# Six more seven-product groups, gates and casts on GpSimd, and a written-out priority table in a fused attention and gated-MLP kernel

## Chip, cores and metric

The kernel runs on one core of a Trainium2 chip. The metric is the time of one execution on the device, in microseconds (us). A ratio is the time of the changed kernel over the time of the kernel before.

## What is computed

Linear attention with a cosine reweighting, then a two-layer network whose gate is h cos(h). Inputs are float32; the kernel computes in float16 and accumulates in float32.

```python
# q, k, v: (8 batches, 8 heads, 576 tokens, 64)
def phi(x, c, s):
    r = np.maximum(x, 0.0)
    return np.concatenate([r * c, r * s], axis=-1)
q_p = phi(q, cos_w, sin_w)
k_p = phi(k, cos_w, sin_w)
kv = np.einsum('bhsf,bhsd->bhfd', k_p, v)
z = np.sum(k_p, axis=2)
num = np.einsum('bhsf,bhfd->bhsd', q_p, kv)
den = np.einsum('bhsf,bhf->bhs', q_p, z)[..., None] + 1e-06
x = num / den          # as 4608 tokens x 512
h = x @ w_in           # 512 -> 2048
out = (h * np.cos(h)) @ w_out   # 2048 -> 512
```

## The kernel before

**Stages.** The 4608 tokens are worked in nine chunks of 512: chunk c below 8 takes 512 tokens of batch c, and the last, chunk 8, collects the 64 left over of each batch. For a chunk there are three stages. `attention(c)` (L1061) loads k, q and v, scales and rectifies them (`prep`, L419 on ScalarE or L420 on VectorE), casts v to float16 (`cast_v`, L433 or L434), multiplies (L446, L507) and normalises (`norm`, L523 to L527). `layer1(c)` (L584) multiplies by w_in and gates. `layer2(c)` (L864) multiplies by w_out; its TensorE work runs interleaved with `layer1(c + 1)`. Chunks 0 and 1 use plain forms of layer 1 (L604), chunk 0 also of layer 2 (L834).

**A plain group of layer 1** (`layer1_plain`, L630) is four tiles of 128 hidden units by 512 tokens. Each tile is four matmuls 512 wide (L636) into one PSUM bank and a `gate`: ScalarE takes the sine of h plus pi/2 (L577), and VectorE multiplies it by the bank (L579).

**A seven-product group** (`layer1_fast`, L708) makes the same four tiles as a 2x2 block product with seven block products instead of eight. Each product is four matmuls 256 wide (L740), so a group has 28 of them against 16 of twice the width. It needs sums of w_in blocks (`w_in_sums`, L669, VectorE) and of x blocks (`layer1_sums`, L689, VectorE). Partial results leave PSUM by three ScalarE copies (L748) into SBUF tiles Y, U and Z and three VectorE additions onto them (L752). Y is gated from SBUF (L577, L579). U and Z are gated together, 1024 wide, from SBUF (L763, L769). The fourth tile is gated from PSUM. `FAST1` (L643) says how many of the four groups of a chunk are done so: two in each of chunks 3 to 8, twelve groups in all. A second set of w_in sums, for groups 2 and 3, is made only if some chunk has more than two (`LATE`, L652); it lies in the buffers of qT.

**Layer 2 from chunk 1 on** is also a seven-product scheme (L897), with sums of the gated tiles on VectorE (L879, L924), copies on ScalarE (L908) and additions on VectorE (L912). In the last chunk the seventh product goes on accumulating in bank A, and at the end ScalarE copies one half of that bank (L943) and VectorE the other (L945), both under one key, and `store` sends the two halves of the tokens from the SP and ACT queues.

**What sets the order.** Every step is given to `Plan` (L18) with an engine, a cost, a due time and the keys that it reads and writes. `Plan.run` (L73) repeats a forward list schedule over the costs (`forward`, L110) and a backward pass that makes new priorities from it, with random changes, and keeps the shortest. The instructions are then issued in the order of the planned starts; each engine works its own in that order, and waits are by semaphores. Steps marked `port=True` (the SBUF sums, `prep`, `cast_v`, gates that name an engine) are kept apart in the plan between VectorE and GpSimd (`held`, `other`, L125 to L132); at run time nothing but the order does this. A gate or `mul` takes VectorE or, with `pool` true, GpSimd (L564). `Y_POOL` and `UZ_POOL` (L645) are empty, so no gate is on GpSimd, and the plan prices one there at 3.4 times the VectorE cost (L569).

**GpSimd's queue** carries the loads of w_in (L976) and w_out (L990), tiny copies that hold back a load until another tensor has landed (L970, L980, L995, L1002), and the output stores (L803) of chunks 0 to 7, each waiting for its rows. `hold2` (L979) keeps the first half of w_out back until the second quarter of w_in has landed.

Of the kernel before, what the change touches and what calls it, by code (L numbers as in the profile page):

```python
# [3 lines left out]

# [7 lines left out]
AF = mybir.ActivationFunctionType  # L12
# [2 lines left out]
F16 = mybir.dt.float16  # L15


class Plan:  # L18

    LINK = {"PE": 0.12, "ACT": 0.05, "DVE": 0.05, "POOL": 0.1, "SP": 0.0}

    PASSES, ROUNDS = 12, 117  # L30


    SHARE, WAKE, LAND = {"HW": 0.40, "SW": 0.56}, {"HW": 1.1, "SW": 1.3}, 1.0
# [7 lines left out]

    def add(self, eng, occ, lat, due, fn, rd=(), wr=(), dma=None, lane=None, late=0.0,
            lazy=None, port=False):

        n = len(self.steps)
        prev = self.lanes.get(lane)
        if lane is not None:  # L50
            self.lanes[lane] = n
        deps = set()
        for key in rd:
            if key in self.wr:
                deps.add(self.wr[key])
        for key in wr:
            if key in self.wr:
                deps.add(self.wr[key])
            deps.update(self.rd.get(key, ()))
        for key in rd:  # L60
            self.rd.setdefault(key, []).append(n)
        for key in wr:
            self.wr[key] = n
            self.rd[key] = []
        deps.discard(n)
        opts = [(eng, occ, lat, fn)] if isinstance(eng, str) else eng
        self.steps.append(dict(opts={o[0]: o for o in opts}, due=due,
                               deps=deps, dma=dma, n=n, prev=prev, late=late,
                               lazy=lazy, port=port))
        self.steps[n].update(zip(("eng", "occ", "lat", "fn"), opts[0]))  # L70
        return n

    def run(self):  # L73

        best = [math.inf]
        rnd = random.Random(1)

        def passes(key, n):
            local = None
            for _ in range(n):
                start, done = self.forward(key)
                end = max(done)
                if end < best[0]:
                    best[:] = [end, start, done, [s["eng"] for s in self.steps]]
                key = self.backward(start, done, end)
                if local is None or end < local[0]:
                    local = end, key  # L90
            return local
        now = passes([s["due"] for s in self.steps], self.PASSES)
        for _ in range(self.ROUNDS):
            amp, wide = rnd.choice((0.5, 1, 2, 4)), rnd.choice((20, 40, 80, 300))
            mid = rnd.uniform(0, best[0])
            key = [k + (rnd.gauss(0, amp) if abs(k - mid) < wide / 2 else 0) for k in now[1]]
            new = passes(key, 4)
            if new[0] < now[0] + 0.02:
                now = new
        for s, a, b, e in zip(self.steps, *best[1:]):  # L100
            s["start"], s["end"] = a, b
            s.update(zip(("eng", "occ", "lat", "fn"), s["opts"][e]))
        return sorted(self.steps, key=lambda s: (s["start"], s["n"]))

    def link(self, n, u):
        st = self.steps
# [3 lines left out]
    def forward(self, key):  # L110
# [103 lines left out]
                late = wake + (self.BUSY if r == "HW" and rings["SW"] and not rings["HW"] else 0.0)  # L214
                rings[r].append([late, s["dma"][0] / s["dma"][1], n, wake])
        return start, done

    def backward(self, start, done, end):
        st = self.steps
        left = [0] * len(st)  # L220
        for s in st:
            for d in s["deps"]:
                left[d] += 1
            if s["prev"] is not None:
                left[s["prev"]] += 1
        limit = [end - done[n] + start[n] for n in range(len(st))]
        late = [0.0] * len(st)
        free = {e: end for e in self.LINK}
        ready = {e: [] for e in self.LINK}
        for n, k in enumerate(left):  # L230
            if not k:
                ready[st[n]["eng"]].append(n)
        for _ in st:
            best = None
            for e, cand in ready.items():
                if not cand:
                    continue
                at = {n: min(free[e], limit[n] + st[n]["occ"]) for n in cand}
                top = max(at.values()) - self.PATIENCE.get(e, 0.0)
                k, t, n = max((start[n], at[n], n) for n in cand if at[n] >= top)  # L240
                if best is None or t > best[0]:
                    best = (t, e, n)
            t, e, n = best
            ready[e].remove(n)
            late[n] = free[e] = t - st[n]["occ"]
            for d in st[n]["deps"]:
                limit[d] = min(limit[d], late[n] - self.link(d, n) - (done[d] - start[d]))
                left[d] -= 1
                if not left[d]:
                    ready[st[d]["eng"]].append(d)  # L250
            d = st[n]["prev"]
            if d is not None:
                limit[d] = min(limit[d], late[n] - 0.01)
                left[d] -= 1
                if not left[d]:
                    ready[st[d]["eng"]].append(d)
        return late


@with_exitstack  # L260
def kernel(
# [162 lines left out]
    def cast_v(b, t, eng, due, hs=slice(0, H), nt=1):  # L424
# [4 lines left out]
            in_ = raw["v"][:, :, t:t + nt, :]  # L429
        rd, wr = hk("v", heads), [("V1", t + i, h) for h in heads for i in range(nt)]  # L430
        f = nt * len(heads) / H
        cost = {"DVE": 0.09 + 0.33 * f, "ACT": 0.12 + 0.5 * f, "POOL": 0.9}
        fn = {"ACT": lambda: nc.scalar.activation(out=out_, in_=in_, func=AF.Copy),  # L433
              "DVE": lambda: nc.vector.tensor_copy(out=out_, in_=in_),  # L434
              "POOL": lambda: nc.gpsimd.tensor_copy(out=out_, in_=in_)}
# [128 lines left out]
    def mul(due, cost, fn, rd, wr, pool):  # L564

        if pool is None:
            dve(cost, due, lambda: fn(nc.vector), rd, wr)
        elif pool:
            pl.add("POOL", 3.4 * cost, 0.15 + 3.4 * cost, due, lambda: fn(nc.gpsimd), rd, wr,  # L569
                   port=True)  # L570
        else:
            dve(cost, due, lambda: fn(nc.vector), rd, wr, port=True)
# [67 lines left out]
             rd=["KQ"] if c == B else [])  # L640


    FAST1 = {3: 2, 4: 2, 5: 2, 6: 2, 7: 2, 8: 2}  # L643
    SUMS_AT = min(FAST1) - 1
    Y_POOL, UZ_POOL = (), ()  # L645
    CH2, JF = NCT // 2, JH * P // 2


# [156 lines left out]
    def store(c, h, o, due, fs=None):  # L805
        O = ost[o]
        keys = [("ost", o, f) for f in range(2)]
        if c < B:
# [2 lines left out]
            put(due, five[:, 2 * h:2 * h + 2, :], blocks(O, n), keys, nc.gpsimd, "POOL")  # L811
            put(due, four[:, 2 * h:2 * h + 2, :], blocks(O, 1 - n), keys, nc.gpsimd, "POOL")
            return
        for n in range(2):
            f = slice(0, Dm) if fs is None else slice(fs * MH, (fs + 1) * MH)
            dst = out.rearrange("(i n s) m -> n i s m", n=2, s=S)[n][2 * h:2 * h + 2, 0:S5, f]
            put(due, dst.rearrange("i (p t) m -> p t i m", t=NT + 1)[:, NT], blocks(O, n)[:, :, f],
                keys if fs is None else [("ost", o, fs)],
                *((nc.scalar, "ACT") if n else (nc.sync, "SP")), nb=262.0 if fs is None else 131.0)

    def layer2_plain(c):

# [41 lines left out]
    def layer2(c):  # L864
# [22 lines left out]
        C_ = Bk if c < B else BANKS[2]  # L887
        order = iter(range(1, 8))

        def product(bank, a, b, rd, first, last):  # L890
            n = next(order)
            for tt in range(2):
                due = w0 + (n - 0.5 + 0.5 * tt) / 7 * ww * 0.97

                def mm(tt=tt):
                    for j in range(JH):
                        nc.tensor.matmul(  # L897
                            bank[0][:, tt * MH:(tt + 1) * MH], lhsT=a[:, j, tt * P:(tt + 1) * P],
                            rhs=b[:, j, :], start=(first and tt == 0 and j == 0),
                            stop=(last and tt == 1 and j == JH - 1), skip_group_check=True)  # L900
                pe(JH, MMH, due, mm, rd, [bank[1]])
            return due

# [31 lines left out]
        store(c, 0, ol, d + 1.5)  # L935
        if c == B:
            store(c, 1, oh, d + 1.0, 1)
        d = product(A, a22, T4, gk(1, 1) + ["T4"], False, True)
        if c < B:
            copy(ost[oh][:, :, m0], A, [("ost", oh, 0)], d + 0.5)  # L940
            store(c, 1, oh, d + 1.5)
        else:
            act(0.3, d, lambda: nc.scalar.activation(  # L943
                out=ost[oh][:, 0, m0], in_=view(A)[:, 0], func=AF.Copy), [A[1]], [("ost", oh, 0)])
            dve(0.33, d, lambda: nc.vector.tensor_copy(  # L945
                out=ost[oh][:, 1, m0], in_=view(A)[:, 1]), [A[1]], [("ost", oh, 0)])
            store(c, 1, oh, d + 1.0, 0)


    def setup():  # L950
        nc.gpsimd.memset(S2[:, 0:2, :], 0.5)
# [16 lines left out]
    def weights():  # L968
# [10 lines left out]
        def hold2():  # L979
            nc.gpsimd.tensor_copy(  # L980
                out=w_out_sb[0:1, :, 0].rearrange("p (g j) -> p g j", g=4)[:, :, 0],
                in_=w_in_sb[0:1, 0, Dff // 4:Dff // 4 + 1].broadcast_to((1, 4)))
        if W_FIRST is None:
            pl.add("POOL", 0.2, 0.3, 0, hold2, [("w_in", 1)], [("w_out", g) for g in range(4)])
            w_out_load(0, 2)

    def w_out_load(g0, g1):
        for g in range(g0, g1):
            js = slice(g * NJT // 4, (g + 1) * NJT // 4)
            pl.add("POOL", 0.9, 0, 0, lambda js=js: nc.gpsimd.dma_start(  # L990
                out=w_out_sb[:, js, :], in_=wo[:, js, :]), (), [("w_out", g)], dma=(1048.0, 400.0), late=LATE_W)

    def hold_raw(nm):
        for h in (0, HB) if nm == ORDER1[2] else (0,):
# [66 lines left out]
    def attention(b):  # L1061
# [4 lines left out]
            for g in range(2):  # L1066
                prep(b, "k", t, g, "", T + 1.2 * t)
        for t, nt in ((0, 2), (2, 2), (4, 1)):
            cast_v(b, t, "", T + 6 + 0.4 * t, nt=nt)
        kv(b, T + 8)  # L1070
        for t in range(NT + 1):
            due = T + 8 + 1.2 * t
# [71 lines left out]
```

## Time and profile before

| | |
|---|---|
| median of 3 timed runs | 285.62 us (284.65 to 286.38) |
| span of the profiled execution | 282.8 us |
| median less span | 2.8 us |
| PE, DVE, ACT, POOL busy | 272.4, 247.5, 215.5, 26.0 us |
| PE, DVE, ACT busy from 105 to 200 us | 94.9, 91.5, 89.3 of 95 us |
| PE busy from 0 to 60 us | 54.7 of 60 us |
| last matmul ends | 277.93 us |
| last store lands | 281.34 us |

The span runs from the first to the last instruction of one execution. The profile gives no time of that execution beyond its span, so the 2.8 us between span and median are carried over as they are. PE is TensorE's matmuls, PEld its weight loads, DVE VectorE, ACT ScalarE, POOL GpSimd, SP the queue that issues most loads. A line "L636 PE MATMUL out<-in shapes x184 | 45.9, 379 | 0.0" reads: line 636 of the code, 184 instructions recorded, 45.9 us busy, 379 ns each, and the idle time of the engine ahead of them. A PE matmul's duration includes the pipeline, so matmuls overlap; the rate at which they pass is read from rows of the timeline or the chain that hold several in one piece. A few matmul records are missing from the trace.

### The profile page before, as it was taken

The numbers are of one execution on the slowest core, as the hardware profiler recorded it, in microseconds if no ns is written. First come the engines' busy times: TensorE is split into PE (matmuls) and PEld (weight loads), VectorE is DVE, ScalarE is ACT, GpSimd is POOL, SyncE is SP. The second block draws the span as 40 slices with busy tenths as digits, with TensorE's granted clock in tenths as the row PEclk, the third lists the DMA queues.
The fourth block names the chain that finished last, engine by engine and source line by source line (L and its number), as shares of the span: only waits on it lengthen the run. The fifth ranks groups of instructions, "written<-read, shape, count | busy, mean of one in ns | idle before, by whom it ended". The sixth has DMA issues, their size and how long they took to land.

```text
span 282.8 us, 6578 instructions
## 1 busy us (share of the span) xinstructions
PE 272.4 (96%) x2619; PEld 208.3 (74%) x2619; DVE 247.5 (88%) x458; ACT 215.5 (76%) x367; POOL 26.0 (9%) x53
## 2 busy tenths in 40 slices
PE   7889989999999999999999999999999999999993
PEld 2468856669866688777877887787777877876882
DVE  2986878999999999999999999999899999967941
ACT  2947897999999999999999999995834666456420
POOL 1412020011000020002000200020002001100200
PEclk9999999999999999999999999999999999999999
DMA  6999999799989999999997899786024001100124
GB/s 214 303 204 273 258 310 300 251 270 212 344 222 240 228 227 362 170 245 224 254 268 186 265 290 224 164 159 167 2 56 168 21 2 75 76 2 0 68 82 150
DMA packets 77567, 53.30 MB, mean 188 GB/s; under 512 B 46048, under 2 KB 75232, under 8 KB 77536
## 3 DMA queue, kind: packets, MB, share of 16 engines
q1 hardware_dynamic: 70032, 39.73, 55.7%
q0 software_dynamic: 6784, 12.59, 17.1%
q10 hardware_dynamic: 720, 0.57, 0.6%
q8 instruction: 20, 0.33, 0.5%
q14 instruction: 11, 0.09, 0.1%
HBM read 36.74 MB, written 9.44 MB: 163 GB/s over the span
## 4 chain that ended last, share of the span: by engine, by line
PE 84%; DMA 8%; ACT 3%; DVE 2%; issue 1%; SPq 0%; ACTq 0%; DVEq 0%
PE M L897 33%; PE M L636 16%; PE M L740 8%; PE M L604 8%; PE TR L740 4%; PE M L834 4%; DMA vm<-in_v_dram 4%; PE TR L636 3%; PE ATT L507 3%; DMA qT<-KQ 3%; PE ATT L446 3%; DMA qm<-in_q_dram 2%; ACT KQ L419 1%; PE M L475 1%; DVE x L527 1%
## 5 line engine op out<-in xcount | busy, mean ns | idle before, releaser
L577 ACT ACTIVATE ch<-M 128x512 f32<-128x512 f32 x90 | 52.8, 595 | 11.1 <-PE M L604 4.1
L897 PEld LDWEIGHTS <-gT 128*128 128x128 f16 x560 | 53.7, 98 | 9.3
L579 DVE TENSOR_TENSOR gT<-M,ch 128x512 f16<-128x512 f32 x83 | 55.4, 683 | 4.7 <-ACT ch L577 4.2
L897 PE MATMUL M<-w_out_sb,gT 128*128 128x256 f16 x448 | 54.9, 273 | 0.0
L636 PE MATMUL M<-xT,w_in_sb 128*128 128x512 f16 x184 | 45.9, 379 | 0.0
L419 ACT ACTIVATE KQ<-qm,CS 128x512 f16<-128x512 f32 x59 | 40.1, 718 | 4.5 <-DMA qm<-in_q_dram 4.5
L419 ACT ACTIVATE KQ<-km,CS 128x512 f16<-128x512 f32 x56 | 38.3, 719 | 0.0
L636 PEld LDWEIGHTS <-w_in_sb 128*128 128x128 f16 x256 | 24.4, 98 | 18.3
L803 POOL DMA_DIRECT2D out_dram<-ost x32 | 17.0, 537 | 213.9 <-DVE ost L912 134.8
L897 PE MATMUL M<-T,S 128*128 128x256 f16 x256 | 32.5, 273 | 0.0
L604 PE MATMUL M<-xT,w_in_sb 128*128 128x256 f16 x256 | 30.6, 273 | 0.1
L897 PEld LDWEIGHTS <-S 128*128 128x128 f16 x256 | 24.9, 98 | 4.0
L604 PEld LDWEIGHTS <-w_in_sb 128*128 128x128 f16 x256 | 24.5, 98 | 3.9 <-issue 0.3
L908 ACT ACTIVATE ost<-M 128x512 f32<-128x512 f32 x31 | 18.5, 597 | 10.2 <-PE M L897 10.1
L527 DVE TENSOR_TENSOR x<-ATT,rec 128x512 f16<-128x512 f32 x32 | 22.1, 691 | 1.1
L740 PEld LDWEIGHTS <-w_in_sb 128*128 128x128 f16 x192 | 18.5, 98 | 4.9 <-issue 0.2
L912 DVE TENSOR_TENSOR ost<-M,ost 128x512 f32<-128x512 f32 x24 | 16.4, 681 | 4.0 <-issue 3.5
L507 PEld LDWEIGHTS <-qT 128*128 128x128 f16 x320 | 15.1, 98 | 4.7 <-issue 0.5
L752 DVE TENSOR_TENSOR Z<-M,Z 128x512 f32<-128x512 f32 x23 | 15.6, 684 | 2.3 <-PE M L740 1.9
L879 DVE TENSOR_TENSOR S<-gT 128x2048 f16<-128x2048 f16 (+1 forms) x16 | 17.3, 1085 | 0.2
L748 ACT ACTIVATE Z<-M 128x512 f32<-128x512 f32 x19 | 11.3, 596 | 6.6 <-PE M L740 6.4
L740 PEld LDWEIGHTS <-WS 128*128 128x128 f16 x144 | 13.6, 98 | 3.3 <-issue 0.2
(130 smaller groups left out, 421.8 us busy)
## 6 DMA issues: line engine op xcount, KB each, us to landing
out_dram<-ost POOLq DMA_DIRECT2D x32, 256.0 KB, 4.3
qm<-in_q_dram SPq DMA_DIRECT2D x8, 640.0 KB, 5.8
km<-in_k_dram SPq DMA_DIRECT2D x8, 640.0 KB, 7.8
qm<-in_q_dram SPq DMA_DIRECT2D x8, 512.0 KB, 5.6
km<-in_k_dram SPq DMA_DIRECT2D x8, 512.0 KB, 6.7
vm<-in_v_dram SPq DMA_DIRECT2D x6, 640.0 KB, 6.4
vm<-in_v_dram SPq DMA_DIRECT2D x6, 512.0 KB, 5.9
w_in_sb<-in_moe_w_in_dram POOLq DMA_DIRECT2D x4, 512.0 KB, 8.9
```

The costliest lines, as they stand in the source:

```text
L419: fn = {"ACT": lambda: nc.scalar.activation(out=out_, in_=in_, func=AF.Relu, scale=sc), "DVE": lambda: nc.vector.tensor_scalar(out=out_, i ...
L507: nc.tensor.matmul(bank[hb][:, hh * D1:(hh + 1) * D1], lhsT=a[:, h, :], rhs=z[:, h, :], start=(i == 0), stop=(i == len(parts) - 1))
L527: nc.vector.tensor_tensor(out=split(x16[n][:, hs, :], k), in0=A[:, :, :, 0:D], in1=split(rec[n][:, hs], k).unsqueeze(3).broadcast_to((P, k ...
L577: act(0.5, due, lambda: nc.scalar.activation(out=ch[c], in_=bank, func=AF.Sin, bias=math.pi / 2.0, scale=1.0), [key], [("ch", c)])
L579: mul(due, 0.61, lambda q: q.tensor_tensor(out=dst, in0=bank if len(dst.shape) == 2 else bank.rearrange("p (j s) -> p j s", j=dst.shape[1] ...
L604: nc.tensor.matmul(M1[m][:, jj * 2 * P:(jj + 1) * 2 * P], lhsT=w_in_sb[:, cc, j * P:(j + 1) * P], rhs=X[:, cc, ts], start=(cc == 0), stop= ...
L636: nc.tensor.matmul(M, lhsT=w_in_sb[:, cc, j * P:(j + 1) * P], rhs=X[:, cc, :], start=(cc == 0), stop=(cc == NCT - 1))
L740: nc.tensor.matmul(bank[0][:, j * TH:(j + 1) * TH], lhsT=a(cc, j), rhs=b[:, cc, :], start=(first and j == 0 and cc == 0), stop=(last and j ...
L803: pl.add(eng, 0.9 if eng == "POOL" else 0.65, 0, due, lambda: q.dma_start(out=dst, in_=src_), keys, [], dma=(nb, 355.0))
L879: dve(0.07 + 1.07 / NG, due, lambda: nc.vector.tensor_tensor(out=out_[:, sl], in0=a[:, sl], in1=b[:, sl], op=op), rd, wr, port=True)
L897: nc.tensor.matmul(bank[0][:, tt * MH:(tt + 1) * MH], lhsT=a[:, j, tt * P:(tt + 1) * P], rhs=b[:, j, :], start=(first and tt == 0 and j == 0),
L908: act(0.5, due, lambda: nc.scalar.activation(out=dst, in_=view(bank), func=AF.Copy), [bank[1]], dk)
```

## The change

- `FAST1` has two groups in chunks 2 to 6 and four in chunks 7 and 8: eighteen instead of twelve. So the first w_in sums are made one chunk earlier (`SUMS_AT`), and the second set (`LATE`) is made.
- `Y_POOL` and `UZ_POOL` name chunks 2 to 8: the gate of Y (512 wide) and that of U and Z (1024 wide) of all eighteen groups go to GpSimd. The plan's price of such a step changes.
- `cast_v` of batches 2 to 7 goes to GpSimd, eighteen casts.
- In the last chunk the seventh product goes to the two banks of BANKS2, one for each half of the tokens, after a ScalarE copy of what bank A holds; VectorE adds each bank to the copy, and `store_tile` sends each half by itself.
- `hold2` waits for the first quarter of w_in, and the plan takes a later landing for w_out.
- The search is gone: `run` makes one forward schedule from a written-out table `KEYS` of priorities, one for each step.

```diff
+KEYS = (
...
+)
     def run(self):
...
+        st = self.steps
+        assert len(KEYS) == len(st)
+        start, done = self.forward([k / 100 for k in KEYS])
+        for s, a, b in zip(st, start, done):
             s["start"], s["end"] = a, b
-            s.update(zip(("eng", "occ", "lat", "fn"), s["opts"][e]))
-        return sorted(self.steps, key=lambda s: (s["start"], s["n"]))
+        return sorted(st, key=lambda s: (s["start"], s["n"]))
...
-        cost = {"DVE": 0.09 + 0.33 * f, "ACT": 0.12 + 0.5 * f, "POOL": 0.9}
+        cost = {"DVE": 0.09 + 0.33 * f, "ACT": 0.12 + 0.5 * f, "POOL": 0.1 + 0.5 * f}
...
-            pl.add("POOL", 3.4 * cost, 0.15 + 3.4 * cost, due, lambda: fn(nc.gpsimd), rd, wr,
+            pl.add("POOL", 0.15 + 1.9 * cost, 0.3 + 1.9 * cost, due, lambda: fn(nc.gpsimd), rd, wr,
                    port=True)
...
-    FAST1 = {3: 2, 4: 2, 5: 2, 6: 2, 7: 2, 8: 2}
+    FAST1 = {2:2,3:2,4:2,5:2,6:2,7:4,8:4}
     SUMS_AT = min(FAST1) - 1
-    Y_POOL, UZ_POOL = (), ()
+    Y_POOL, UZ_POOL = range(2, 9), range(2, 9)
...
+    def store_tile(o, i, due):
+        for n in range(2):
+            dst = out.rearrange("(i n s) m -> n i s m", n=2, s=S)[n][2 + i, 0:S5, 0:MH]
+            put(due, dst.rearrange("(p t) m -> p t m", t=NT + 1)[:, NT], blocks(ost[o], n)[:, i, 0:MH],
+                [("ost", o, 0, i)], *((nc.scalar, "ACT") if n else (nc.sync, "SP")), nb=65.5)
...
-        d = product(A, a22, T4, gk(1, 1) + ["T4"], False, True)
         if c < B:
+            d = product(A, a22, T4, gk(1, 1) + ["T4"], False, True)
             copy(ost[oh][:, :, m0], A, [("ost", oh, 0)], d + 0.5)
             store(c, 1, oh, d + 1.5)
-        else:
-            act(0.3, d, lambda: nc.scalar.activation(
-                out=ost[oh][:, 0, m0], in_=view(A)[:, 0], func=AF.Copy), [A[1]], [("ost", oh, 0)])
-            dve(0.33, d, lambda: nc.vector.tensor_copy(
-                out=ost[oh][:, 1, m0], in_=view(A)[:, 1]), [A[1]], [("ost", oh, 0)])
-            store(c, 1, oh, d + 1.0, 0)
-
+            return
+        copy(ost[oh][:, :, m0], A, [("ost", oh, 0, i) for i in range(2)], d + 0.5)
+        d = product(BANKS2, a22, T4, gk(1, 1) + ["T4"], True, True, True)
+        for i, (bank, key) in enumerate(BANKS2):
+            dst = ost[oh][:, i, m0]
+            dve(0.33, d, lambda dst=dst, bank=bank, i=i: nc.vector.tensor_tensor(
+                out=dst, in0=bank[:, i * MH:(i + 1) * MH], in1=dst, op=ALU.add), [key, ("ost", oh, 0, i)],
+                [("ost", oh, 0, i)])
+            store_tile(oh, i, d + 1.0)
...
-                in_=w_in_sb[0:1, 0, Dff // 4:Dff // 4 + 1].broadcast_to((1, 4)))
+                in_=w_in_sb[0:1, 0, 0:1].broadcast_to((1, 4)))
         if W_FIRST is None:
-            pl.add("POOL", 0.2, 0.3, 0, hold2, [("w_in", 1)], [("w_out", g) for g in range(4)])
+            pl.add("POOL", 0.2, 0.3, 0, hold2, [("w_in", 0)], [("w_out", g) for g in range(4)])
...
-                out=w_out_sb[:, js, :], in_=wo[:, js, :]), (), [("w_out", g)], dma=(1048.0, 400.0), late=LATE_W)
+                out=w_out_sb[:, js, :], in_=wo[:, js, :]), (), [("w_out", g)], dma=(1048.0, 400.0), late=1.8)
...
-            cast_v(b, t, "", T + 6 + 0.4 * t, nt=nt)
+            cast_v(b, t, "POOL", T + 6 + 0.4 * t, nt=nt)
```

## Prediction

> **What bounds the kernel now.** I read the page's busy times first, then busy times by stretch, then the chain of waits through a middle stretch. The two lines from the page:
>
> ```profile
> PE 272.4 (96%) x2619; PEld 208.3 (74%) x2619; DVE 247.5 (88%) x458; ACT 215.5 (76%) x367; POOL 26.0 (9%) x53
> PEclk9999999999999999999999999999999999999999
> ```
>
> Three engines are near full, so shares don't decide. The clock is full throughout. Busy time by stretch (length, then PE, PEld, DVE, ACT, POOL):
>
> ```profile
> 0.00:60.00 60.00, 54.74 (x540) 38.12 (x541) 47.04 (x111) 44.36 (x77) 10.09 (x23) 1.00 1.01 261
> ...
> 105.00:200.00 95.00, 94.89 (x952) 75.53 (x950) 91.52 (x158) 89.32 (x152) 6.35 (x12) 1.00 0.91 224
> ...
> 222.00:250.00 28.00, 28.00 (x229) 22.19 (x228) 25.50 (x43) 15.97 (x28) 2.11 (x4) 1.00 0.13 44
> 250.00:278.00 28.00, 27.93 (x227) 21.96 (x225) 19.77 (x30) 12.64 (x22) 2.12 (x4) 1.00 0.12 46
> ```
>
> PE is idle for 5.3 us up to 60 us and hardly at all later, while VectorE stands at 96% from 105 to 200 us and ScalarE at 94%. Busy matmuls overlap, so I check the rate in the chain (start, length, what; PE work alone here):
>
> ```profile
> 130.56 0.87 PE M L897 x8
> 131.43 1.21 PE ATT L446 x40
> 132.64 1.75 PE M L897 x16
> 134.39 0.87 PE M L740 x8
> ...
> 145.36 1.73 PE M L636 x8
> ```
>
> Each piece starts where the one before ends. A matmul 256 wide passes in 0.87 / 8 = 0.109 us, one 512 wide in 1.73 / 8 = 0.216. TensorE runs at its own rate without holes from 60 to 277.9 us. So matmul work that goes away is time, as long as the other engines keep up.
>
> **The change part by part.** The sum is made against the profiled span, 282.8 us. The median of the runs is 285.62, so 2.8 us are added at the end unchanged.
>
> **Six more seven-product groups.** One plain group is 16 matmuls of 0.216 = 3.46 us; one seven-product group is 28 of 0.109 = 3.05. That is 0.40 us less each, 2.4 us for six, all on the full TensorE stream. Gain: **2.4 us**.
>
> Beside it, ScalarE does three copies (0.60 each), the sines of Y (0.63) and of UZ (1.06) and one sine from PSUM (0.59), 4.1 us, against four sines of 0.595, 2.4 us: 1.7 more per group, 10 in all. Two groups fall in chunk 2 (about 80 to 105 us, where ScalarE is busy 24.1 of 25) and four after 200 us, where it has 40% and more free. VectorE does three additions (0.684) and one gate (0.683) against four gates: no change, if Y and UZ are gated elsewhere.
>
> **Gates to GpSimd.** These rows show what leaves VectorE, and GpSimd's nearest row:
>
> ```profile
> L769 DVE TENSOR_TENSOR gT<-Z,ch 128x1024 f16<-128x1024 f32 x9 | 10.9, 1217 | 0.1
> ...
> L579 DVE TENSOR_TENSOR gT<-Z,ch 128x512 f16<-128x512 f32 x9 | 6.1, 682 | 0.0
> ...
> L951 POOL MEMSET S<- 128x512 f16 x1 | 0.5, 524 | 0.3 <-POOLq L1128 0.3
> ```
>
> With the three of each in other buffers, twelve groups free 12 x (1.22 + 0.68) = 22.8 us of VectorE. No row has a two-input product on GpSimd. Its floor is VectorE's own time, 0.68 and 1.22 us. For the upper end I take one memset for each of the two inputs and the output: 3 x 0.52 = 1.6 us for Y and 3.1 for UZ. I take the upper end, since the memset is GpSimd's only wide row. Eighteen groups are then 18 x 4.7 = 85 us.
>
> [...]
>
> **Casts to GpSimd.** Twelve of 1024 and six of 512 leave ScalarE (8.5 + 2.5 = 11.0 us) and VectorE (2.7 + 0.8 = 3.5). On GpSimd, one memset each for input and output: 2.1 and 1.05 us as upper end, 0.69 and 0.42 (VectorE's rows) as floor. At most 31 us. With 17 us of stores GpSimd has 133 us of the 200 from chunk 2 on, and in chunks 7 and 8 four groups take 19 us of the 8 x 3.05 = 24.4 us that TensorE needs for a chunk (four groups and as much again in layer 2). It doesn't become the bound by its own work.
>
> These moves gain nothing by themselves: VectorE hides behind TensorE already. They are the cover of the 2.4 us. VectorE ends near 247.5 - 22.8 - 3.5 + 2.7 (second w_in sums, 4 x 0.68) + 1.7 (x sums of chunk 2) = 225.6 us, and ScalarE where it was (+10 - 11). If that cover fails, the gain is given back at the price under the rivals. What is queued behind a waiting instruction: on GpSimd, gates and casts stand behind stores, which now wait 0.7 to 3.1 us for the second pair of a chunk; behind a late gate stand VectorE's sums L879 of layer 2, and behind those, in order, its additions that empty PSUM.
>
> **Earlier w_in sums.** Four sums of 0.68 move from chunk 3 to chunk 2 and must follow the last use of the plain block, near 76 us. TensorE has layer 2 of chunk 1 (112 x 0.109 = 12.2 us) and the two plain groups of chunk 2 (6.9 us) to do meanwhile: nothing. Without that cover, 2.7 us.
>
> **Tail.** The end now:
>
> ```profile
> 277.96 0.38 ACT L943 ACTIVATE ost<-M 128x256 f32<-128x256 f32 x1 [4.77 <-PE M L897]
> 278.38 0.42 DVE L945 COPY ost<-M 128x256 f32<-128x256 f32 x1 [1.60 <-ACT ost L943]
> 278.84 0.64 ACTq L803 DMA_DIRECT2D out_dram<-ost  x1
> ```
>
> The two halves of one bank are emptied one after the other, and the last store goes out 0.91 us after the last matmul (277.93). With a bank for each half, the first half is added and sent while the second is multiplied (8 x 0.109 = 0.87 us). After the last matmul stand one addition of 0.42 us (as L527's 128x256 row) and two hops of some 0.03: the store goes out at +0.49, **0.4 us** earlier. The first half's store then occupies the queue from -0.38 for 0.64 to 0.77 us, to +0.39 at most, just clear. The half-size transfer may land up to 0.3 us sooner, or the queue cost 0.3; I take neither. The added copy of bank A (0.60) hides under the last two products (3.5 us).
>
> **`hold2` and w_out.** The first half of w_out would be asked for at about 20 us instead of 24.25, but the fourth quarter of w_in, ahead of it on the same queue, lands at 28.0: nothing. The hold for the second q load, behind those issues on GpSimd, can go 2 us earlier (23.9 for 25.72). Loads ahead of it on SP's queue land until 29.5, so I take nothing; at best it takes away TensorE's waits between 41.8 and 43.5 us, 1.1 us in all, at worst the loads share the same bandwidth and cost that much.
>
> **The table.** It decides only the order. No row prices it. TensorE has no holes after 60 us to win; before that at most the 1.1 us above and the 0.9 us it waits for w_out at 37 us. A worse order could cost as much. I take 0.
>
> Sum: 282.8 - 2.4 - 0.4 = 280.0 us of span; with 2.8, **282.7 us**, 1.0% faster.
>
> **The rivals.**
>
> *The head gains as well* (0.10): loads and order take 1.3 of the 2.0 us of waits near 37 and 42 us. For it: those waits are on transfers that the change lets out earlier. Against: the transfers are full there (1.01 of 16 engines). 281.4 us.
>
> *Given back by order* (0.18): a group takes longer to finish on GpSimd (UZ 3.1 against 1.22 us), and where layer 2's sums wait for the last group of a chunk, TensorE runs out of other work. At the last chunk there are only the first two products (3.5 us) as cover. Some 0.3 us at each of six boundaries is 1.8: 284.5 us, no measurable change.
>
> *Slower: VectorE and GpSimd shut each other out of SBUF* (0.17). The code plans the steps apart, but only by order. After the change VectorE has 13 such steps a chunk (4 sums of layer 2 at 1.22, 4 x sums at 0.42, some 5 preparations at 0.48: 9 us of 27), GpSimd up to 12 us of 27. If a VectorE step stands behind a UZ gate of up to 3.1 us, two half products (1.74 us) cover it, and TensorE loses up to 1.4. It decides once TensorE loses 2.8 us in all, 0.16 us for each of 18 UZ gates. With four of the 18 colliding fully it loses 5.6: 288.3; with two, 285.5. For it: VectorE was at 96% with no reserve, and no row shows the two together. Against: 22.8 us of reserve are new, and the order leaves each step some room.
>
> The Trainium skill (SBUF — State Buffer, SBUF: two separate sides) speaks for this rival: GpSimd and a VectorE step with two SBUF inputs take one pair of ports exclusively, for the whole instruction. By that rule the additions L752 and L912 and the gates from PSUM stay free. No run here shows it.
>
> *The change doesn't do what it says* (0.05): ScalarE, 24.1 of 25 us busy around chunk 2, takes the 3.4 us of two groups there without getting the casts' time back, and stops TensorE for most of it: 285.3 us.
>
> **How the numbers follow.** The forecast has 0.50, with 282.0 to 283.7 as its own range. A measurement of this kernel can tell about 0.5% (1.4 us) from no change. Faster: forecast and head, 0.60, and a little of the third, 0.02: 0.62. Same: the rest of it, the last rival and a mild collision, 0.23. Slower: 0.15. The range runs from the head rival with a sooner-landing tail, 280.8, to 287.0, which takes in three full collisions (4.2 us).
>
> **What would show it.** Right: 18 groups in L740 (504 matmuls of 256), PE busy near 268 to 270 us with no idle time from 60 us to the end, VectorE near 226 us, POOL between 80 and 150 us, one addition between the last matmul and the last store. Wrong: PE waits on VectorE or ScalarE after 60 us, L879 or L420 longer than now (1.22 and 0.48 us), idle VectorE time that ends with a POOL gate, or UZ gates over 3.1 us.

## The result and the profile after

The changed kernel takes **292.84 us** (291.83 to 293.54, median of 4 runs) against 286.00 (284.65 to 286.98) for the kernel before on the same chip: a ratio of **1.0244**, 95% interval 1.0211 to 1.0277. It is slower by 2.4%, where I forecast 1.0% faster, and it lies outside the range.

The page of the kernel after, busy times and granted clock:

```profile
PE 273.0 (94%) x2691; PEld 216.2 (74%) x2691; DVE 250.7 (86%) x443; ACT 209.9 (72%) x361; POOL 115.0 (39%) x107
PEclk9999999999999999999999999999999999979998
```

GpSimd took 115 us, within the forecast 80 to 150. But VectorE, from which twelve groups' gates and six casts went away, is busier than before (250.7 against 247.5 us) where I expected 225.6. The same stretches as before (length, then PE, PEld, DVE, ACT, POOL, granted clock):

```profile
0.00:60.00 60.00, 54.64 (x539) 37.77 (x540) 46.79 (x113) 44.14 (x78) 11.48 (x24) 1.00 1.03 263
...
105.00:200.00 95.00, 90.78 (x908) 71.51 (x905) 90.67 (x147) 78.47 (x136) 42.78 (x37) 1.00 0.98 226
...
222.00:250.00 28.00, 26.94 (x248) 24.00 (x246) 24.65 (x40) 19.95 (x34) 16.57 (x11) 1.00 0.08 25
250.00:278.00 28.00, 25.30 (x217) 21.81 (x216) 21.47 (x29) 13.87 (x23) 17.35 (x13) 0.94 0.12 47
```

Up to 60 us nothing has changed. After that PE, which had hardly been idle, is idle for 4.2 us of the middle stretch and 2.7 of the last. VectorE has 11 instructions fewer between 105 and 200 us and is busy for nearly the same time (90.7 against 91.5 us), so single instructions must have become longer. The groups of instructions, shapes kept apart, show which (line, engine, operation, tiles, count, busy us, mean ns, idle before):

```profile
L604 DVE TENSOR_TENSOR gT<-M,ch 128x512 f16<-128x512 f32 x71 | 47.2, 684 | 5.8 <-ACT ch L602 5.0
L794 POOL TENSOR_TENSOR gT<-Z,ch 128x1024 f16<-128x1024 f32 x11 | 26.4, 2401 | 35.4 <-ACT ch L788 35.4
...
L604 POOL TENSOR_TENSOR gT<-Z,ch 128x512 f16<-128x512 f32 x11 | 16.6, 1513 | 39.2 <-ACT ch L602 39.2
L445 DVE TENSOR_SCALAR KQ<-km,CS 128x512 f16<-128x512 f32 x27 | 16.4, 644 | 1.5 <-DMA km<-in_k_dram 1.5
...
L722 DVE TENSOR_TENSOR XS<-xT,XS 128x512 f16<-128x512 f16 x10 | 7.2, 717 | 0.1
L912 DVE TENSOR_TENSOR S<-gT 128x1024 f16<-128x1024 f16 x4 | 6.3, 1598 | 0.0
```

The same groups in the kernel before:

```profile
L579 DVE TENSOR_TENSOR gT<-M,ch 128x512 f16<-128x512 f32 x83 | 55.4, 683 | 4.7 <-ACT ch L577 4.2
...
L420 DVE TENSOR_SCALAR KQ<-km,CS 128x512 f16<-128x512 f32 x24 | 10.7, 489 | 0.1
...
L697 DVE TENSOR_TENSOR XS<-xT,XS 128x512 f16<-128x512 f16 x8 | 3.4, 420 | 0.1
...
L879 DVE TENSOR_TENSOR S<-gT 128x1024 f16<-128x1024 f16 x4 | 2.7, 684 | 0.0
```

L604 on DVE (L579 before) is the gate with one input in PSUM: 684 ns, 683 before. The last three rows, L445, L722 and L912, are L420, L697 and L879 before, and their means were 489, 420 and 684 ns. They use SBUF alone. The medians of L445 and L722 are still 478 and 420 ns: most instances are as before, and a few take 0.9 to 2.6 us. The clearest place, in the timeline (start, us, engine; brackets give the idle time before and what ended it):

```profile
252.89 1.29 POOL L604 TENSOR_TENSOR KQ<-vm,ch 128x512 f16<-128x512 f32 x1
253.08 3.96 DVE L912 TENSOR_TENSOR S<-gT 128x1024 f16<-128x1024 f16 x1
...
254.13 2.35 POOL L794 TENSOR_TENSOR KQ<-qm,ch 128x1024 f16<-128x1024 f32 x1
...
258.28 0.68 DVE L777 TENSOR_TENSOR Z<-M,Z 128x512 f32<-128x512 f32 x1
...
259.02 0.84 PE L765 MATMUL M<-XS,qT 128*128 128x256 f16 x4 [2.70 <-DVE Z L777]
```

A layer-2 sum of 0.68 us begins while GpSimd gates Y. GpSimd goes straight on to gate U and Z, until 256.48. The sum ends at 257.04, 0.56 after that gate, so most of its work of 0.68 us came only then. Three more VectorE steps stand behind it in order, and the third is the addition that TensorE's next bank waits for: TensorE stands for 2.70 us (2.9 counted from where the matmul before passed at its own rate).

I compared every VectorE instruction after 60 us with the median of its form in the kernel before. **18 of them are stretched, by 21.1 us together**: preparations L445 by 8.8 (7 of 20), x sums L722 by 5.9 (4), layer-2 sums L912 by 4.7 (4), L959 and the w_out sums L890 by 1.7 (3). The gates L604 and additions L777, which read a PSUM bank, lost less than 0.1 us in all, though 31 of the 69 gates and 21 of the 54 additions overlapped a gate or cast on GpSimd.

**Balance** of the two profiled spans (291.7 less 282.8, +8.9): TensorE idle or slowed after 60 us, 12.8 against 0.8 us: +12.0 (9.6 of the 12.8 are seven holes, some 1.7 a stretch at half clock that the last section shows). Matmul work, 264.5 against 267.0 us of matmuls at their own rates: -2.5. Last matmul to end of span, 4.2 against 4.9 us: -0.7. Head: +0.1. That makes +8.9. The medians differ by less, 6.8, as the profiled execution of after was 0.7 above its median and that of before (about 284.6 us by the span) 1.4 below.

### The profile page after: what moved, and what is told of

It is laid out like the page before. It is cut to its first block, busy times and chain, and to the rows that moved or that the text cites. A ratio compares the mean times of both kernels' runs of the same rounds, so it can differ in the third digit from the quotient of the medians.

```text
span 291.7 us, 6815 instructions
## 1 busy us (share of the span) xinstructions
PE 273.0 (94%) x2691; PEld 216.2 (74%) x2691; DVE 250.7 (86%) x443; ACT 209.9 (72%) x361; POOL 115.0 (39%) x107
## 4 chain that ended last, share of the span: by engine, by line
PE 51%; DVE 28%; DMA 11%; issue 5%; ACT 3%; SPq 0%; DVEq 0%; POOL 0%; ACTq 0%
PE M L932 21%; DMA km<-in_k_dram 9%; PE M L765 8%; DVE KQ L445 6%; PE M L661 5%; PE M L629 4%; DVE gT L604 4%; DVE Z L777 3%; PE TR L765 3%; DVE S L912 3%; PE M L867 2%; DVE ost L947 2%; DMA qm<-in_q_dram 2%; ACT ch L602 2%; DVE XS L722 2%
## 5 line engine op out<-in xcount | busy, mean ns | idle before, releaser
L602 ACT ACTIVATE ch<-M 128x512 f32<-128x512 f32 x73 | 42.6, 597 | 16.6 <-DVE gT L604 7.3
L604 DVE TENSOR_TENSOR gT<-M,ch 128x512 f16<-128x512 f32 x71 | 47.2, 684 | 5.8 <-ACT ch L602 5.0
L444 ACT ACTIVATE KQ<-qm,CS 128x512 f16<-128x512 f32 x56 | 37.9, 720 | 4.3 <-DMA qm<-in_q_dram 4.2
L794 POOL TENSOR_TENSOR gT<-Z,ch 128x1024 f16<-128x1024 f32 x11 | 26.4, 2401 | 35.4 <-ACT ch L788 35.4
L444 ACT ACTIVATE KQ<-km,CS 128x512 f16<-128x512 f32 x53 | 36.1, 720 | 0.4 <-DMA km<-in_k_dram 0.4
L661 PE MATMUL M<-xT,w_in_sb 128*128 128x512 f16 x128 | 32.3, 379 | 0.7 <-DVE gT L604 0.5
L604 POOL TENSOR_TENSOR gT<-Z,ch 128x512 f16<-128x512 f32 x11 | 16.6, 1513 | 39.2 <-ACT ch L602 39.2
L460 POOL CAST V<-vm 128x1024 f16<-128x1024 f32 (+1 forms) x18 | 19.4, 1114 | 30.1 <-DMA vm<-in_v_dram 30.1
L777 DVE TENSOR_TENSOR Z<-M,Z 128x512 f32<-128x512 f32 x31 | 20.6, 680 | 1.5 <-ACT ch L602 0.8
L912 DVE TENSOR_TENSOR S<-gT 128x2048 f16<-128x2048 f16 (+1 forms) x16 | 20.9, 1314 | 0.2
```

The costliest lines, as they stand in the source:

```text
L602: act(0.5, due, lambda: nc.scalar.activation(out=ch[c], in_=bank, func=AF.Sin, bias=math.pi / 2.0, scale=1.0), [key], [("ch", c)])
L604: mul(due, 0.61, lambda q: q.tensor_tensor(out=dst, in0=bank if len(dst.shape) == 2 else bank.rearrange("p (j s) -> p j s", j=dst.shape[1] ...
L661: nc.tensor.matmul(M, lhsT=w_in_sb[:, cc, j * P:(j + 1) * P], rhs=X[:, cc, :], start=(cc == 0), stop=(cc == NCT - 1))
L777: dve(0.61, due + 0.3, lambda: nc.vector.tensor_tensor(out=dst, in0=bank[0], in1=dst, op=ALU.add), [bank[1], key], [key])
L794: mul(due, 1.14, lambda q: q.tensor_tensor(out=g4, in0=four(uz), in1=four(cc2), op=ALU.mult), [zk[1], zk[2], *ck], [("g", gi(c), h * JH + ...
L912: dve(0.07 + 1.07 / NG, due, lambda: nc.vector.tensor_tensor(out=out_[:, sl], in0=a[:, sl], in1=b[:, sl], op=op), rd, wr, port=True)
```

## The experiments

**Shut out** is the theory that GpSimd steps that read SBUF hold up VectorE steps that use SBUF alone, and that TensorE then waits behind these. The rivals: **late gates** (a gate takes longer on GpSimd and its consumers wait), **the table** (a bad order) and **the extra groups** (VectorE or ScalarE can't feed them). Each ratio below is to the kernel before on the same chip.

For late gates the trace of the changed kernel itself says little: after 60 us no idle time of PE or of VectorE is put down to a GpSimd step, and ScalarE has two such waits, 1.5 and 0.2 us.

### Short gates, same order

The gates on GpSimd stay where they are, with their waits, but multiply only 8 columns of each tile row; the rest of these tiles is left ungated.

```diff
+            w = 8
+            mul(due, 0.61, lambda q: q.tensor_tensor(
+                out=dst[:, :, 0:w], in0=bank.rearrange("p (j s) -> p j s", j=dst.shape[1])[:, :, 0:w],
...
-                out=g4, in0=four(uz), in1=four(cc2), op=ALU.mult), [zk[1], zk[2], *ck],
+                out=g4[:, :, :, 0:8], in0=four(uz)[:, :, :, 0:8], in1=four(cc2)[:, :, :, 0:8], op=ALU.mult), [zk[1], zk[2], *ck],
```

> The changed kernel with every gate on GpSimd cut to 8 columns of each tile row (the rest of Y, U and Z stays ungated, so that part of the computation is left out). Order, waits and all other instructions stay. Theory 'shut out' (VectorE's steps between SBUF tiles stand while GpSimd works on SBUF, and TensorE runs out of free banks): the stretch of VectorE's SBUF steps falls from 21 us to under 5 us (the casts are left), TensorE's idle time after 60 us from 13 us to about 2, and the time to 282 to 285 us. Rival 'late gates' (a gate takes longer on GpSimd and the sums wait for it): the same time, so this run does not tell these two apart. Rival 'table' (the written-out order is bad by itself): 290 us or more.

Measured: 285.94 us, ratio 0.9991 (0.9947 to 1.0035), a little above the 282 to 285 us expected; three of the ten runs took 282.6 to 283.0 us, the others 285.8 and more. VectorE's stretch falls from 21.1 to 1.0 us and its busy time to 231.8. In the profiled execution (285.92 us) TensorE stands for 3.15 us in one place:

```profile
181.27 1.33 ACT L444 ACTIVATE KQ<-qm,CS 128x512 f16<-128x512 f32 x2 [3.87 <-DMA qm<-in_q_dram]
...
183.12 0.69 DVE L611 TENSOR_TENSOR gT<-M,ch 128x512 f16<-128x512 f32 x1 [0.98 <-ACT ch L602]
...
183.86 1.07 PE L668 MATMUL M<-xT,w_in_sb 128*128 128x512 f16 x4 [3.15 <-DVE gT L611]
```

ScalarE comes to the preparation of the last q load before the load has landed; the sines stand behind it in order, the gate behind these, TensorE behind the gate. So the time alone decides little here: the stretch is gone, but a second weakness shows. In the table's order the last q load has no slack once the rest runs faster, which is part of the table rival.

### Short gates, as long as before

The same short products, each with two memsets of the rest of its tile behind it, so that GpSimd is held about as long. The gating of those columns is left out.

```diff
...
+                q.tensor_tensor(out=g4[:, :, :, 0:8], in0=four(uz)[:, :, :, 0:8],
+                                in1=four(cc2)[:, :, :, 0:8], op=ALU.mult)
+                for _ in range(2):
+                    q.memset(g4[:, :, :, 8:], 0.25)
```

> As the run with short gates, but each is followed on GpSimd by two memsets of the rest of the destination, so that GpSimd is busy about as long as with the real gates (estimated from the memset row, about 1.1 and 2.0 us) and the sums wait as long, while GpSimd reads hardly anything. 'Late gates': 290 to 293 us with VectorE's steps at their usual lengths. 'Shut out' by any GpSimd work on SBUF: 289 to 293 us with stretched VectorE steps. 'Shut out' only by GpSimd instructions that read SBUF: 283 to 286 us. 'Table': 290 us or more without stretch.

Measured: **282.03 us**, ratio 0.9900 (0.9857 to 0.9943), below even the 283 to 286 us expected for the theory. Page and groups:

```profile
PE 269.8 (96%) x2691; PEld 215.3 (76%) x2691; DVE 234.3 (83%) x443; ACT 210.5 (75%) x361; POOL 106.8 (38%) x179
```

```profile
L809 POOL MEMSET gT<- 128x992 f16 x28 | 26.5, 945 | 0.8
L445 DVE TENSOR_SCALAR KQ<-km,CS 128x512 f16<-128x512 f32 x27 | 15.1, 597 | 1.2 <-DMA km<-in_k_dram 1.2
...
L733 DVE TENSOR_TENSOR XS<-xT,XS 128x512 f16<-128x512 f16 x10 | 4.2, 420 | 0.1
```

GpSimd is busy for 106.8 us against 115.0, in the same order and with the same waits. The two-input sums (L733 is after's L722) are back at 420 ns, the stretch is 4.1 us, 3.4 of it in the preparations, and TensorE idles for 2.8 us after 60 us. **Late gates falls**: from the start of a short product to the end of its second memset it takes 1.24 us for Y and 2.10 for U and Z (medians), against 1.28 and 2.36 for the gates of the changed kernel, so the results come about as late. The table is not what costs the 10.8 us between this run and the changed kernel. What differs is that GpSimd hardly reads SBUF in the gates.

### The search instead of the table

```diff
-        start, done = self.forward([k / 100 for k in KEYS])
```

The list is gone and `Plan.run` searches, as in the kernel before; all else is as after.

> The changed kernel with the search of the kernel before (its passes, rounds and seed) in place of the table. 'Table': 286 us or less. 'Shut out' and 'late gates': 289 to 296 us, with VectorE's SBUF steps stretched as with the table.

Measured: 291.93 us, ratio 1.0239 (1.0185 to 1.0293). Another order, 15.6 us of stretch, and the same time as after. The table is not the cause, and this search over the same plan (one seed) doesn't find a way around it.

### GpSimd work beside the kernel before

The kernel before with 36 extra products of 512 on GpSimd whose result nobody uses, paced by VectorE's gates through a tiny VectorE memset (0.06 us) each.

```diff
+        nc.vector.memset(pace, 1.0)
+        nc.gpsimd.tensor_copy(out=DUM[:, 0:1], in_=pace)
+        for _ in range(n):
+            nc.gpsimd.tensor_tensor(out=DUM, in0=T2.rearrange("p j s -> p (j s)")[:, 0:512],
+                                    in1=T3.rearrange("p j s -> p (j s)")[:, 0:512], op=ALU.mult)
```

> The kernel before with GpSimd work beside it on which nothing waits: after each of the 24 gates from SBUF, which stay on VectorE, GpSimd multiplies two constant 512-wide tiles once (Y) or twice (UZ), 36 products of about 1.3 us, 46 us in all; VectorE writes 24 single columns to pace them. Order and dependences of all else are those of the kernel before. 'Shut out': VectorE's SBUF steps that meet a product get longer by up to the product's length, 8 to 12 us in all, and the time rises by 3 to 6 us, to 289 to 292. 'Late gates' and 'table': 286 to 287 us, no change.

Measured: 288.83 us, ratio **1.0131** (1.0095 to 1.0166).

The control has 84 memsets of 512 in place of the 36 products: it holds GpSimd as long but reads nothing.

```diff
+        for _ in range(5 * n // 2):
+            nc.gpsimd.memset(DUM, 0.5)
```

> The kernel before with the same work beside it, but memsets of the scratch tile in place of the products: 84 memsets of 0.52 us, 44 us in all, with the same 24 pacing columns, so GpSimd is busy as long and only writes. If GpSimd shuts VectorE out only while it reads SBUF: VectorE's sums keep their lengths and the time is that of the kernel before, 285 to 287 us. If any GpSimd work on SBUF does it, or the pacing, or the descriptors of the stores held up on GpSimd: 288 to 290 us as with the products.

Measured: 285.35 us, ratio **0.9981** (0.9953 to 1.0009). The groups, products first, then memsets:

```profile
L716 POOL TENSOR_TENSOR DUM<-T,T 128x512 f16<-128x512 f16 x36 | 42.8, 1190 | 2.9
...
L892 DVE TENSOR_TENSOR S<-gT 128x1024 f16<-128x1024 f16 x4 | 3.6, 913 | 0.0
...
L697 DVE TENSOR_TENSOR XS<-xR 128x512 f16<-128x512 f16 x2 | 2.7, 1329 | 0.0
```

```profile
L716 POOL MEMSET DUM<- 128x512 f16 x84 | 44.5, 529 | 4.9
...
L891 DVE TENSOR_TENSOR S<-gT 128x1024 f16<-128x1024 f16 x4 | 2.7, 684 | 0.0
...
L697 DVE TENSOR_TENSOR XS<-xR 128x512 f16<-128x512 f16 x2 | 0.8, 414 | 0.0
```

GpSimd is held for 42.8 and 44.5 us. Beside the products x sums take 1329 ns where they take 414 beside memsets, and VectorE is stretched by 7.4 us in all against 0.8. No instruction waits for the products, and the control has the same pacing and holds GpSimd as long; what is left to cost the 1.3% is the collisions. PE is idle for 1.9 us between 60 and 278 us beside the products and for 0.4 beside the memsets; 1.3 of the 1.9 are two waits on VectorE's gates, each right behind a stretched sum (230.41 and 241.52 us). This is the mechanism by itself; stretch and time came out just under the 8 to 12 us and 289 to 292 us expected.

### The other parts by themselves

Eighteen groups, tail, `hold2` and search, but all gates on VectorE and the casts where they were (a kernel before with these parts of the diff):

```diff
-    FAST1 = {3: 2, 4: 2, 5: 2, 6: 2, 7: 2, 8: 2}
+    FAST1 = {2:2,3:2,4:2,5:2,6:2,7:4,8:4}
...
```

> The changed kernel without its GpSimd work: eighteen seven-product groups, gates from SBUF on VectorE, v casts on VectorE or ScalarE as before, tail in two banks, search in place of the table. 'Shut out': no stretched VectorE step; VectorE carries 12 to 15 us more than in the kernel before (six groups more at 1.9 us, second w_in sums 2.7), so it may press in chunk 2, and the time is 283 to 287 us, well below the changed kernel. If the eighteen groups themselves cost the time (ScalarE's copies, w_in sums), it stays at 289 us or more.

Measured: 286.08 us, ratio 1.0042 (1.0011 to 1.0074). No stretch; VectorE is at 258.6 us, and TensorE idles 3.4 us between 60 and 100 us, around chunk 2, where ScalarE is busy for 24.9 of the 25 us from 80 to 105. Part of that may be the fourth rival of the prediction, ScalarE without the casts' time back; the trace has one wait of 0.9 us on a copy of it. The extra groups without cover gain nothing.

The same without the six groups, so tail, `hold2` and the later w_out alone:

```diff
...
+        d = product(BANKS2, a22, T4, gk(1, 1) + ["T4"], True, True, True)
+        for i, (bank, key) in enumerate(BANKS2):
...
```

> Twelve groups, gates and casts as before the change, search as before: of the change only the tail in two banks, the earlier hold of w_out and its later planned landing are left. Tail term 0.4 us (0.1 to 0.7): 284.8 to 285.4 us beside 285.5 for the kernel before. A measurement can hardly tell this from no change; the profile can: the last store should go out about 0.5 us after the last matmul instead of 0.9.

Measured: 284.21 us, ratio 0.9942 (0.9916 to 0.9967): 1.4 us less than the kernel before, more than the 0.1 to 0.7 us expected of the tail, and another order may be in it. From the last matmul to the end of the span it is 4.1 us against 4.9.

Without chunk 2's two groups, four each in chunks 7 and 8 (16 groups, gates on VectorE):

```diff
-    FAST1 = {2:2,3:2,4:2,5:2,6:2,7:4,8:4}
+    FAST1 = {3: 2, 4: 2, 5: 2, 6: 2, 7: 4, 8: 4}
```

> As the run with eighteen groups on VectorE, but sixteen: two groups in chunks 3 to 6 and four in chunks 7 and 8, where VectorE and ScalarE have room. 'Shut out': TensorE keeps its stream, 4 x 0.40 and the tail come off: 283 to 284 us, faster than both kernels. If the seven-product groups do not give their 0.40 us each, 285 us or more.

Measured: 284.65 us, ratio 0.9976 (0.9940 to 1.0012), so not the 283 to 284 us expected and no clear gain. The holes between 60 and 100 us are gone; some 3.5 us of small ones later remain.

The casts alone on GpSimd, in the kernel before:

```diff
-            cast_v(b, t, "", T + 6 + 0.4 * t, nt=nt)
+            cast_v(b, t, "POOL", T + 6 + 0.4 * t, nt=nt)
```

> The kernel before with the eighteen v casts on GpSimd and nothing else (the plan's price of such a cast corrected). 'Shut out': casts read SBUF as the gates do, 18 to 19 us of GpSimd time against some 83 for the whole change; stretch of VectorE's SBUF steps 1 to 4 us, time 285 to 287 us. If the gates alone shut VectorE out, no stretch and 285 us or less.

Measured: 287.79 us, ratio 1.0062 (1.0021 to 1.0104). Both expectations missed: the time is higher than either, and only one VectorE step is stretched, by 0.14 us, so the small loss is not the shut-out; the search finds another order, with 1.6 us of TensorE idle between 60 and 72 us. How much another order can move the time by chance, the next one samples once: the kernel before with another seed of its search.

```diff
-        rnd = random.Random(1)
+        rnd = random.Random(2)
```

> The kernel before with another seed of its search, nothing else: how much a different order moves the time by itself. 'Shut out' and 'late gates' say nothing; if orders from this search differ by over 1%, the gains and losses of about 1% in the runs that search anew can't be put down to their edit alone. Expected 284 to 288 us.

Measured: 286.12 us, ratio 1.0003 (0.9969 to 1.0037). One other order is within 0.4% of the first. Ratios nearer to 1 than that, of kernels with a search of their own, I don't read as effects; one seed bounds this only loosely.

### Only Y's gate on GpSimd

Eighteen groups with tail, `hold2` and search, Y's gate on GpSimd, the longer one of U and Z and the casts as before:

```diff
...
-    Y_POOL, UZ_POOL = (), ()
+    Y_POOL, UZ_POOL = range(2, 9), ()
...
```

> Eighteen groups with only the 512-wide gate of Y on GpSimd (18 of 1.3 us, 23 us), the gates of U and Z on VectorE, casts as before the change, search, tail in two banks. 'Shut out' with the wait as its size: a VectorE step waits at most 1.3 us, within the 1.7 us that two half products of TensorE cover, so little is lost: stretch 2 to 7 us, 283 to 286 us. If any GpSimd gate costs its full length on TensorE: 288 us or more.

Measured: 287.06 us, ratio 1.0026 (0.9988 to 1.0063), above the 283 to 286 us expected. The stretch is 3.4 us, VectorE at 254.7; TensorE idles for 3.3 us from 60 to 100 us again. The same with 16 groups, none in chunk 2:

```diff
-    FAST1 = {2:2,3:2,4:2,5:2,6:2,7:4,8:4}
+    FAST1 = {3: 2, 4: 2, 5: 2, 6: 2, 7: 4, 8: 4}
```

> As the last, with sixteen groups (two in chunks 3 to 6, four in chunks 7 and 8): 283 to 285 us if the cover of 1.7 us holds; 287 us or more if not.

Measured: **282.20 us**, ratio **0.9878** (0.9848 to 0.9908), faster than both kernels and than the 283 to 285 us expected. Its page:

```profile
PE 270.9 (96%) x2667; PEld 213.2 (76%) x2667; DVE 249.1 (89%) x455; ACT 219.6 (78%) x375; POOL 48.7 (17%) x69
```

The stretch is 1.8 us and TensorE idles for 1.4 us after 60 us. By this trace it has the cover that the changed kernel meant to make, with the gate of 1.3 us on GpSimd and not the one of 2.4. That the gate's move is what pays is not shown: against the same sixteen groups with all gates on VectorE (0.9976) it is 1% faster, in another order, but the same move on eighteen groups gained nothing (1.0026 beside 1.0042).

## Why the prediction was wrong, point by point

- **Six more groups, -2.4 us: right.** All 504 half-width products are there, and matmul work fell by 2.5 us. It was gained in the work and lost in waits.
- **Earlier w_in sums, 0: right.** The three sums left after 60 us stand at 76.27, 78.89 and 83.49 us. PE is busy for all of the 20 us from 60 to 80 us, and its one hole before 105 us stands behind a stretched w_out sum (92.20 us).
- **Tail, -0.4: right in sign, a little small.** Last matmul to end is 0.7 us shorter. The second addition ends 0.47 us after the last matmul, as the working had it.
- **`hold2` and w_out, 0; table, 0: nothing seen against them in the head** (PE busy up to 60 us differs by 0.1). With the search in place of the table the time is the same. That the last q load has no slack in the table's order shows only where the rest runs faster: with short gates, and with the paced ones, where ScalarE waits 2.2 us for it and TensorE 1.5 soon after. In the changed kernel that load lands at 180.84 us, 3.2 us before ScalarE comes to it.
- **GpSimd's price: inside the bounds.** Y 1.28 and U with Z 2.36 us (medians), between 0.68 and 1.6 and between 1.22 and 3.1; GpSimd didn't become the bound. Some took up to 1.88 and 3.11: GpSimd waits for VectorE as well (these two, at 84.56 and 235.36 us, began while a layer-2 sum with two SBUF inputs ran on VectorE).
- **The failed step** is the one that costs the gates and casts at nothing: "These moves gain nothing by themselves ... They are the cover of the 2.4 us", with VectorE near 225.6 us. The cover was 22.8 us of freed VectorE time, and the stretch, which the sum has at nothing, ate 21.1 of it; TensorE, which was to have no idle time, lost 9.6 us in holes and some 1.7 at half clock. With six more preparations that the order gave VectorE (6 x 0.48 = 2.9) and the second addition of the tail (0.4), 225.6 comes to 250.0; measured 250.7.
- **The rival that came true** is the shut-out, to which I gave 0.17. Its place was right (sums L879, x sums L697 and preparations L420 before; PSUM readers free). Its size was not: I let at most four of 18 gates collide fully, with 1.4 us of TensorE time each, so 288.3 us. There were 18 stretched steps, and TensorE had seven holes of 0.5 to 2.9 us, 9.6 us together (six of them right behind a stretched step, five of these beside gates and one beside casts; the one of 0.5 us without one). The price of one full collision was near 1.4 us by luck. In four places a step was held for 2.1 to 2.2 us beyond its own length, less than the 3.1 of the working, and TensorE still stood for 1.0 to 1.7 us, so the cover was 0.4 to 1.1 us and not 1.74. Once a step stood through both gates of a group (3.96 us), which the working did not have, and that cost 2.9 us and the clock. VectorE works in order, so the late step takes along the additions and gates behind it, which empty banks that TensorE needs. "The order leaves each step some room" was an argument from the plan, which holds the steps apart by its own costs; nothing holds them apart when the real times differ.
- **Where the weighing failed:** the point from which the rival decides was 0.16 us per U and Z gate. At 96% of VectorE and about 9 us of SBUF steps and 12 us of GpSimd in 27, an order that isn't held to makes several overlaps a chunk likely (18 steps in seven chunks were stretched). By these numbers the rival deserved more than 0.17; how much more, no run shows.
- **The base** mixed two things: each execution of the changed kernel lies about 1.8 us above its own span, so of the 2.8 us about 1 is that the profiled execution of the kernel before was faster than the median. For a forecast of a median the sum is the same, and it changes nothing in the sign.

Where the loss comes from: with GpSimd held as long but hardly reading, the changed kernel takes 282.0 us, close to the forecast 282.7. That the loss comes with GpSimd's reading of SBUF is shown from both sides, by taking it from the changed kernel and by adding it to the kernel before.

The Trainium skill (SBUF — State Buffer, SBUF: two separate sides) says that the pair of ports goes to whoever starts first, and that VectorE asks for it with two SBUF inputs only against a GpSimd step that reads, but in its two-port modes against any. The traces agree on the sums, which stayed at 420 ns beside memsets. The one-input preparations took up to 1.34 us for 0.48 there (one took 1.22 beside a memset alone), as the page would have it if they run in a two-port mode; no run here shows the mode.

How the 21.1 us split can be read from what GpSimd was doing beside each stretched step: 14.9 us stood beside gates, 4.0 beside a gate with a cast behind it, and 2.0 beside casts alone (three steps, at 92.20, 155.96 and 178.61 us). So most of it is the gates'; no run takes the casts alone out of the changed kernel.

Not settled: why 18 groups with Y on GpSimd are no better than with all gates on VectorE. The holes around chunk 2 point to that stretch, and nothing was tested further.

## What to carry to other kernels

Before work goes to GpSimd, count VectorE's steps without a PSUM input in the same stretch and set the length of one GpSimd step, and of two in a row, against what the bound engine has as cover; the freed time counts only after that. A plan's order is no lock: where two engines must not meet, make the steps short, or give them a real wait (which no run here tried). Here all gates and casts on GpSimd cost 2.4% (1.0244); the kernel with sixteen groups, the new tail and only the gates of 1.3 us there took 0.9878, of which the gates' own share is open.

## What the runs showed of the hardware

- A VectorE step can stand through two GpSimd steps in a row: 3.96 us for 0.68, as shown above, and 0.94 for 0.48 behind two casts at 155.96 us. It need not: at 92.20, 116.39, 178.61 and 236.17 us of the same trace the VectorE step got in behind the first of two adjoining GpSimd steps, and the second then took longer.
- A hole of 2.9 us was enough to lose TensorE's clock. Three stretches of the changed kernel's trace around the hole at 259 us (columns as above; the number behind POOL's is the granted clock):

```profile
257.00:259.00 2.00, 0.00 (x0) 0.00 (x0) 1.97 (x5) 0.00 (x0) 0.00 (x0) 1.00 0.00 0
259.00:260.50 1.50, 1.48 (x8) 1.07 (x8) 0.56 (x1) 1.11 (x2) 0.73 (x1) 0.57 0.02 5
260.50:262.00 1.50, 1.50 (x8) 1.03 (x7) 0.33 (x1) 1.25 (x3) 0.53 (x1) 0.50 0.00 0
```

  The clock is granted in full through the hole and then halved for some 3.4 us; sixteen matmuls passed 0.1 us late each, 1.7 us on top of the 2.9. The same came after 3.3 us in the kernel with short gates and after 2.3 us in the one with the search (granted 1.00 from 176 to 178.6 us, 0.79 to 180, 0.50 to 182), and not after 2.0 us there (239.69 us) or 1.7 us here (119.61). The Trainium skill (TensorE: Matmul & The Clock Gate, HAM oscillation) speaks of gaps above about 3.4 us; here 2.3 was enough.
